# Hashed attention and a gated FFN on one core: turns, hashes, value products and means cut into products and laid out over the slots of the opening; later loads in another order

## The chip, the cores and the metric

The kernel runs on one core of a Trainium2 chip. The metric is the device time of one execution in microseconds (us), from a few runs of the same program; one further execution was taken by the hardware profiler, and every row below is from that one.

## What is computed

The first stage is attention for 4 batches of 8 heads, 768 tokens of 64 numbers, in which a query sees only the keys of its own hash bucket. The second is a feed-forward network with a gate over the 3072 tokens, all in float32:

```python
q_bits = (np.einsum('bhsd,dk->bhsk', q, proj) > 0)       # proj: 64 x 6
k_bits = (np.einsum('bhsd,dk->bhsk', k, proj) > 0)
...
mask = q_bucket[:, :, :, None] == k_bucket[:, :, None, :]
scores = np.where(mask, scale * np.matmul(q, k.transpose(0, 1, 3, 2)), -1e9)
...
attn = attn / (np.sum(attn, axis=-1, keepdims=True) + 1e-09)
x = np.matmul(attn, v)                                   # then heads side by side: 3072 x 512
...
xn = x / np.sqrt(np.mean(x * x, axis=-1, keepdims=True) + 1e-06) * rms_g
g = xn @ w_gate                                          # 512 x 1536
out = (g * sigmoid(g) * (xn @ w_val)) @ w_out            # 1536 x 512
```

## The kernel before

**Windows and slots.** A window w is half of a batch (batch w // 2): 384 queries of all 8 heads. The work is laid out by hand over slots. A slot is one third of one head in one window: scores of 256 keys against the 384 queries (`scores`, two products, L338) and their exponential on ScalarE (`probs`, L349). `SLOTS` (L34) lists them. The first 48 belong to windows 0 and 1, pair of heads by pair of heads in the order of `TURNS` (L33): pair 0 of window 0, pair 0 of window 1, pair 1 of window 0, and so on, except that pairs 2 and 3 of window 0 come before pairs 2 and 3 of window 1. From slot 48 on windows 2 to 7 follow, 24 slots each. Scores have two buffers in PSUM (`scps`).

**The plan.** `at(s, f, ..., rank)` puts a step into slot s. The last loop (L699) emits for each slot s the scores of slot s + 1, the steps of rank under 3, the exponential of slot s + 1, then the other steps by rank and order of entry. Every engine and every DMA queue works through its own instructions in the order in which they were emitted; SyncE's queue carries nearly all loads of q, k and v and the small moves of hash bits, and in the later part the output.

**Preparing a head.** Batch 0 and pairs 0 and 1 of batch 1 (`BY_PE`, L40) are turned by TensorE: `turn_pe` (L161) makes three 128x128 products into one PSUM bank, DVE copies the bank to `kT` or `qT` (`keep`), POOL and ScalarE cast it into `QK` (`casts`, L543). Pairs 2 and 3 of batch 1 and all of batches 2 and 3 are loaded in blocks (`load_blocks`, four DMAs) and turned on DVE (`turn_dve`, L187, four instructions each for k and q) and cast on POOL (`cast_pool`). The hash of two heads is one group of four float32 products of 384 columns, side by side on TensorE (`hash_bank`, L206), followed by one sign operation on DVE (`signs`) that gives +-16 and +-32 in `bits`. Twelve rows of bits per block then go under the 64 rows of the head in `QK` (so that the mask is part of the score product): by DVE copies or by small DMAs on SyncE. `hash_head` (L231) hashes one head of batch 0, `hash_heads` (L253) a pair, `hash_lone` (L273) pairs 2 and 3 of batch 1, with eight moves on SyncE each.

**Values, means, normalization.** `av` (L357) multiplies the exponentials with the values, 18 products a head, in halves of nine in the second and third slot after the head. `v_prep` casts the values; `v_sum` and `v_mean` (L319) give the mean of the values that stands in for the 1e-9. `attn_out` (L374) divides, `sumsq`, `norm`, `scale_x` (L420) and `turn_x` (L425) normalize and turn x. For window 0 this comes at slots 38 to 47, since the network of window 0 begins in slot 48.

**The network.** Twelve `gate` and `value` groups of four products in 16 slots, then `project`. Turns, hashes, means, x turns, gates, values and projections share three PSUM banks (`gps`, tag "g"); each bank is freed by the engine that reads it, DVE for most.

**Loads.** Ten tiles for raw q, k and v (`lpool`). The opening's loads of batch 0 stand ahead of the slots, among them the v of pairs 2 and 3 (L566, L567). The weights are loaded and cast by DMAs of POOL's queue (`load_w`, `load_wo`) in slots 2 to 39.

Of the kernel before, what the change touches and what calls it, by code (L numbers as in the profile page):

```python
# [36 lines left out]
LAST = {(w, h): g for g, (w, h, p) in enumerate(SLOTS) if p == 2}  # L37

# [5 lines left out]
def kernel(  # L44
# [115 lines left out]

    def turn_pe(b, h, which, room=None):  # L161
        hp, hh = divmod(h, 2)
        qk_tile(b, hp)
        if hh == 0:
            t_tile(b, hp, which)
        src = raw[b, hp, which][:, hh].rearrange("p (c e) d -> p c (e d)", e=2)
        ps = bank("t_ps", [128, HALF]) if room is None else room
        for i in range(3):
            nc.tensor.transpose(ps[:, 128 * i : 128 * i + 128], src[:, i], ident)  # L169
        return ps  # L170
# [82 lines left out]
    def hash_heads(b, hp):  # L253

        ps = hash_bank(
            [(w[:, 0:32], t0(b, 2 * hp + hh, which))
             for hh in range(2) for w, which in ((pk, "k"), (pq, "q"))]
        )
        bt = bits_tile(0)
        signs(bt, ps)  # L260

        def move(eng, blocks):
            for hh, t in blocks:
                p0 = 64 * hh + 32 * (t % 2) + 12 * (t // 2)
                dst, src = bit_rows(b, 2 * hp + hh, t), bt[p0 : p0 + 12]
                if eng is nc.sync:
                    eng.dma_start(out=dst, in_=src)  # L267
                else:
                    eng.tensor_copy(dst, src)

        return move
# [47 lines left out]
    def v_mean(b, hp, n, parts=(None,)):  # L319
        hs = slice(2 * hp, 2 * hp + n)  # L320
        ps = bank("m_ps", [128, n, 65])
        for i, jt in enumerate(parts):
            rhs = vsum[b % 2][:, hs, 0:65] if jt is None else vls[b % 2][:, hs, jt, 0:65]
            nc.tensor.matmul(
                ps, ones16, rhs, start=(i == 0), stop=(i == len(parts) - 1)
            )
        nc.vector.tensor_scalar_mul(cvb[b % 2][:, hs, 0:65], ps, C0 / S)
# [29 lines left out]
    def av(w, h, i0, i1):  # L357
# [5 lines left out]
        for i in range(i0, i1):  # L363
            c, jt = divmod(i, 6)
            nc.tensor.matmul(  # L365
                o[:, c, hh, 0:65],
                psb[w, h][:, jt // 2, jt % 2, 128 * c : 128 * c + 128],
                vls[b % 2][:, h, v_chunk(b, h, jt), 0:65],
                start=(hh == 0 and i == 0), stop=(jt == 5),
                skip_group_check=True,  # L370
            )
# [48 lines left out]
    def scale_x(w, c):  # L420
        if w not in xn:
            xn[w] = npool.tile([128, 3, DMODEL], FP16, name="xn")
        nc.vector.tensor_scalar_mul(xn[w][:, c, :], x[w][:, c, :], rstds[w][:, c : c + 1])  # L423
# [142 lines left out]
    load_rows(nc.sync, 0, 2, "v")  # L566
    load_rows(nc.sync, 0, 3, "v")  # L567
# [13 lines left out]
    def hash_one(h):  # L581
        moves[h] = hash_head(h)
        moves[h]((nc.sync,), 3)

    def hash_pair(b, hp):
        moves[b, hp] = hash_heads(b, hp)
        odd = [(0, 2), (1, 2), (0, 3), (1, 3)]
        even = [(0, 0), (0, 1), (1, 0), (1, 1)]
        moves[b, hp](nc.sync, odd if b == 0 else even[:2] + odd[:1] + even[2:] + odd[1:])

# [4 lines left out]
    for hp, turns, sv in ((1, (1, 2, 4, 5), 8), (2, (8, 9, 10, 11), 19), (3, (14, 15, 17, 18), 25)):  # L595
        for i, s in enumerate(turns):
            at(s, keep_pair, 0, hp, i)
            at(s + 1, casts, 0, hp, i)
        at(sv, v_prep, 0, hp)

    for h, s in ((2, 3), (3, 7)):
        at(s, hash_one, h)
        for t in range(3):
            at(s + 1 + t, lambda h=h, t=t: moves[h]((nc.vector,), t), rank=5)
    for hp, s, slots in ((2, 13, (15, 16, 17, 18)), (3, 20, (22, 23, 24, 25))):
        at(s, hash_pair, 0, hp)
        for i, s in enumerate(slots):
            at(s, lambda hp=hp, i=i: moves[0, hp](nc.vector, [divmod(i, 2)]), rank=5)
    for hp, s in enumerate((6, 16, 30, 36)):
        at(s, v_mean, 0, hp, 2, range(6))  # L610
    for i, (t, src) in enumerate(((wg, moe_w_gate), (wv, moe_w_val))):
        at(2 + 4 * i, load_w, t, src, 0, 768)
        at(12 + 9 * i, load_w, t, src, 768, 1536)
        at(33 + 6 * i, load_wo, 6 * i, 6 * i + 6)

    for hp, loads, turns, sv in ((0, (9, 11, 15), (24, 26, 28, 30), 42),
                                 (1, (13, 17, 28), (33, 35, 37, 39), 45)):
        for which, s in zip("kqv", loads):  # L620
            at(s, load_rows, nc.sync, 1, hp, which)
        for i, s in enumerate(turns):
            at(s, keep_pair, 1, hp, i)
            at(s + 1, casts, 1, hp, i)
        at(turns[3] + 2, hash_pair, 1, hp)
        at(sv, v_prep, 1, hp)
        at(sv + 2, v_sum, 1, hp)
# [3 lines left out]
    def in_row(loads, s, hash_slot=None):  # L631
# [3 lines left out]
        (1, 2): ((21, 23, 30), (36, 37, 40, 40, 48, 49, 50, 51), (42, 52, 46), 53),  # L635
        (1, 3): in_row((42, 44, 47), 52, 61),
        (2, 0): in_row((51, 56, 59), 61), (2, 1): in_row((64, 67, 70), 71, 80),
# [20 lines left out]
    at(54, v_mean, 1, 0, 4)  # L658
# [16 lines left out]
    for w in range(8):  # L675
        for h in range(H):
            end = LAST[w, h] + 3
            at(end - 1, av, w, h, 0, 9)
            at(end, av, w, h, 9, 18)
            if h % 2:  # L680
                at(end, o_step, w, h // 2, rank=4.5)
                if (w, h) != (0, 7):
                    at(end + 6, s_step, w, h // 2, rank=5)
        at(end + (1 if w == 0 else 9), norm, w, rank=5)
        for c in range(3):
            at(end + (3 if w == 0 else 14 + c), scale_x, w, c, rank=5)
            at(end + (7 + c if w == 0 else 17 + 2 * c), turn_x, w, c, rank=1)
# [70 lines left out]
```

## Time and profile before

| | us |
|---|---|
| median of 3 runs | 339.33 (337.27, 339.33, 345.63) |
| the profiled execution | 339.3 |
| its span | 337.5 |
| TensorE busy in the span | 326.8 |
| DVE / ScalarE / POOL busy | 236.4 / 210.0 / 155.3 |

A row of the timeline gives start, duration, engine, line, operation, result and operands, shape and count, and in brackets how long the engine was idle before it and what ended that. Rows of equal instructions that follow each other are merged (x4). The ends of matmuls are modelled, so that the distance from one start to the next tells more than the duration. "SPq" is the queue that SyncE issues DMAs from: the duration there is the issuing, not the transfer.

### The profile page before, as it was taken

The page shows a single profiled execution, that of the slowest core. Times are in us where ns is not written, and L with a number is a line of the kernel's source. Part 1 is how long each engine was busy: PE and PEld are TensorE (multiplying, and loading weights), DVE is VectorE, ACT ScalarE, POOL GpSimd, SP SyncE. Part 2 cuts the span into 40 slices and gives each one's busy share as a digit, 9 for nine tenths or more (in the row PEclk, how much of TensorE's full clock was granted, in tenths as well). Part 3 has the DMA queues.
Part 4 walks back from the last instruction along what each step waited for, and adds up shares of the span by engine and source line. Part 5 has one row for each costly group of instructions (what it writes and reads, how often), then busy time and mean ns, then how long its engine had stood idle before and what let it go on. Part 6 is the DMA issues. An engine that isn't in the chain of part 4 may idle for free.

```text
span 337.5 us, 7796 instructions
## 1 busy us (share of the span) xinstructions
PE 326.8 (97%) x2993; PEld 201.0 (60%) x2993; DVE 236.4 (70%) x526; ACT 210.0 (62%) x328; POOL 155.3 (46%) x230
## 2 busy tenths in 40 slices
PE   8999989889999999999999999999999999999995
PEld 7566656455566565566555666566556665655653
DVE  4769798688758896668768897557546663883860
ACT  3789987656666575757666676567667675332321
POOL 4878789836465576245736475613111311110000
PEclk9999999999999999999999999999999999999999
DMA  7999999464376064508243261100010001001002
GB/s 238 330 223 260 169 169 187 75 124 100 79 186 118 15 111 119 104 20 168 69 105 84 44 116 64 35 16 0 33 62 2 3 0 64 33 0 64 32 0 93
DMA packets 80244, 31.36 MB, mean 93 GB/s; under 512 B 65240, under 2 KB 77264, under 8 KB 80208
## 3 DMA queue, kind: packets, MB, share of 16 engines
q1 hardware_dynamic: 76272, 26.09, 31.7%
q0 software_dynamic: 3712, 4.72, 8.8%
q8 instruction: 23, 0.38, 0.5%
q14 instruction: 13, 0.11, 0.1%
q10 hardware_dynamic: 224, 0.07, 0.1%
HBM read 28.32 MB, written 6.29 MB: 103 GB/s over the span
## 4 chain that ended last, share of the span: by engine, by line
PE 85%; DVE 6%; SPq 3%; DMA 2%; ACT 2%; issue 1%; DVEq 0%; ACTq 0%
PE y_ps L469 18%; PE v_ps L455 17%; PE s_ps L343 15%; PE g_ps L445 12%; PE o_ps L365 9%; PE s_ps L445 5%; PE d_ps L209 4%; SPq L267 2%; PE t_ps L169 1%; PE x_ps L430 1%; PE z_ps L336 1%; DMA kL<-in_k_dram 1%; DVE otmp L380 1%; DVE xn L423 1%; ACT psb L353 1%
## 5 line engine op out<-in xcount | busy, mean ns | idle before, releaser
L353 ACT ACTIVATE psb<-s_ps 128x768 f16<-128x768 f32 x192 | 150.8, 808 | 28.1 <-PE s_ps L343 26.9
L343 PE MATMUL s_ps<-QK 76*128 76x384 f16 x384 | 93.5, 325 | 1.3 <-ACT psb L353 0.5
L455 PE MATMUL v_ps<-xnT,wv 128*128 128x384 f16 x384 | 78.1, 326 | 0.1
L469 PE MATMUL y_ps<-wo,ht 128*128 128x512 f16 x276 | 69.2, 379 | 0.3 <-ACT ysb L476 0.3
L389 POOL TENSOR_TENSOR x<-otmp,rcp 128x384 f32<-128x384 f32 x31 | 25.7, 830 | 93.0 <-DVE rcp L385 92.7
L365 PEld LDWEIGHTS <-psb 128*128 128x128 f16 x1152 | 51.6, 97 | 25.5 <-issue 7.5
L447 ACT ACTIVATE t<-g_ps 128x384 f32<-128x384 f32 x72 | 35.3, 490 | 43.6 <-PE g_ps L445 43.4
L458 DVE SCALAR_TENSOR_TENSOR ht<-a,v_ps 128x384 f16<-128x384 f32 x96 | 53.2, 554 | 10.7 <-PE v_ps L455 1.5
L457 DVE SCALAR_TENSOR_TENSOR a<-t,g_ps 128x384 f32<-128x384 f32 x72 | 39.5, 548 | 28.5 <-ACT t L447 28.3
L445 PE MATMUL g_ps<-xnT,wg 128*128 128x384 f16 x288 | 58.6, 325 | 0.7 <-DVE a L457 0.5
L365 PE MATMUL o_ps<-vl,psb 128*128 128x65 f16 x1152 | 56.8, 194 | 0.6 <-DVE otmp L380 0.5
L455 PEld LDWEIGHTS <-wv 128*128 128x128 f16 x384 | 36.4, 97 | 23.9 <-issue 0.5
L445 PEld LDWEIGHTS <-wg 128*128 128x128 f16 x384 | 36.0, 97 | 24.4 <-issue 1.1
L343 PEld LDWEIGHTS <-QK 76*128 76x128 f16 x384 | 31.6, 98 | 16.1 <-issue 3.7
L469 PEld LDWEIGHTS <-ht 128*128 128x128 f16 x276 | 25.9, 97 | 24.0 <-issue 0.6
L476 ACT COPY ysb<-y_ps 128x512 f32<-128x512 f32 x23 | 13.5, 585 | 25.5 <-PE y_ps L469 22.8
L431 DVE TENSOR_TENSOR xnT<-x_ps,gcol 128x512 f16<-128x512 f16 x24 | 16.3, 685 | 15.1 <-PE x_ps L430 15.1
L401 POOL TENSOR_TENSOR sq<-x 128x384 f32<-128x384 f32 x31 | 25.6, 826 | 2.4
L380 DVE TENSOR_TENSOR otmp<-o_ps,cvb 128x390 f32<-128x390 f32 x32 | 17.8, 558 | 8.8 <-PE o_ps L365 8.7
L447 ACT ACTIVATE t<-s_ps 128x384 f32<-128x384 f32 x24 | 11.8, 491 | 18.4 <-PE s_ps L445 17.6
L201 POOL CAST QK<-kT 64x768 f16<-64x768 f32 x20 | 16.8, 838 | 12.4 <-DVE kT L193 6.5
L193 DVE STREAM_TRANSPOSE kT<-kL 128x192 f32<-128x192 f32 x40 | 19.8, 517 | 2.7 <-DMA kL<-in_k_dram 2.7
(80 smaller groups left out, 325.7 us busy)
## 6 DMA issues: line engine op xcount, KB each, us to landing
vL<-in_v_dram SPq DMA_DIRECT2D x16, 384.0 KB
out_dram<-ysb SPq DMA_DIRECT2D x23, 256.0 KB
kL<-in_k_dram SPq DMA_DIRECT2D x40, 96.0 KB
qL<-in_q_dram SPq DMA_DIRECT2D x40, 96.0 KB
kL<-in_k_dram SPq DMA_DIRECT2D x5, 384.0 KB
qL<-in_q_dram SPq DMA_DIRECT2D x5, 384.0 KB
wg<-in_moe_w_gate_dram POOLq DMA_DIRECT2D x2, 768.0 KB, 7.2
wv<-in_moe_w_val_dram POOLq DMA_DIRECT2D x2, 768.0 KB, 8.5
```

The costliest lines, as they stand in the source:

```text
L343: nc.tensor.matmul(ps[:, j, 0:HALF], k_cols(w // 2, h, 2 * p + j), q_cols(w, h), start=True, stop=True,)
L353: nc.scalar.activation(psb[w, h][:, p], sps.pop(g)[:, :, 0:HALF], AF.Exp, scale=ESCALE,)
L365: nc.tensor.matmul(o[:, c, hh, 0:65], psb[w, h][:, jt // 2, jt % 2, 128 * c : 128 * c + 128], vls[b % 2][:, h, v_chunk(b, h, jt), 0:65], s ...
L380: nc.vector.tensor_add(tmp[:, :, :, 0:65], o[:, :, :, 0:65], cvb[b % 2][:, 2 * hp : 2 * hp + 2, 0:65].unsqueeze(1).to_broadcast([128, 3, 2 ...
L389: eng.tensor_mul(xd.rearrange("p c (h d) -> p c h d", h=2), tmp[:, :, :, 0:64], r.to_broadcast([128, 3, 2, 64]),)
L401: nc.gpsimd.tensor_mul(sq, xd, xd)
L445: nc.tensor.matmul(g, wg[:, kt, fs], xnT[w][:, kt], start=(kt == 0), stop=(kt == 3))
L447: nc.scalar.activation(t, g, AF.Tanh, scale=0.5)
L455: nc.tensor.matmul(vv, wv[:, kt, fs], xnT[w][:, kt], start=(kt == 0), stop=(kt == 3))
L457: nc.vector.scalar_tensor_tensor(out=a, in0=t, scalar=1.0, in1=g, op0=ALU.add, op1=ALU.mult)
L458: nc.vector.scalar_tensor_tensor(out=ht[w][:, ft], in0=a, scalar=0.5, in1=vv, op0=ALU.mult, op1=ALU.mult)
L469: nc.tensor.matmul(y, ht[w][:, ft, c * 128 : (c + 1) * 128], wo[:, ft, :], start=(ft == 0), stop=(ft == NF - 1),)
```

## The change

In the opening (slots 0 to 50) pieces take the place of whole steps:

- A turn is made by `turn_part`, product by product; the dictionary `turns` says how many products each slot takes. Pair 1 of batch 1 is turned in slots 39 to 44 (33 to 39 before), pair 0 in slots 27 to 36 (24 to 30).
- A hash is made by `hash_part` in pieces of 128 columns; `hashes` gives for each hash the slots of its three columns. Heads 6 and 7 of batch 0 get a hash each (one for both before). Pairs 0 and 1 of batch 1 are hashed in slots 37 to 39 and 46 to 47 (32 and 41 before).
- `by_dve` names the bit moves that DVE makes and their slots (18, before 14); the others of batch 0 go to SyncE (6, before 10), as do all 16 of batch 1's pairs 0 and 1.
- Means of pairs 1 to 3 of batch 0 are cut in two; values of windows 0 and 1 are multiplied pair by pair in five slots (`av_pair`; four for the last pair of window 0, whose result comes a slot earlier). One of three rows of x of window 0 is scaled on ScalarE.
- Loads: v of pairs 2 and 3 of batch 0 move into slots 17 and 24; q, k, v of batch 1's pairs 0 and 1 from slots 9 to 28 to slots 18 to 40; the output weights from slots 33 and 39 to 47 and 50. Pair 2 of batch 1 is loaded in slots 40, 48, 49 (21, 23, 30 before), turned in 50 to 55 (36 to 51), hashed in 56 (53); pair 3 is loaded in 50, 52, 54 (42, 44, 47), turned in 56 to 61 (52 to 59), hashed in 62 (61); the casts and sums of v go along.

```diff
+    def turn_part(b, h, which, i0, i1):
...
+        ps = tps[b, h, which]
...
+        for i in range(i0, i1):
+            nc.tensor.transpose(ps[:, 128 * i : 128 * i + 128], src[:, i], ident)
+        if i1 == 3:
+            nc.vector.tensor_copy(t0(b, h, which), ps)
...
+    def hash_part(b, heads, i0, i1):
...
+        cs = slice(128 * i0, 128 * i1)
+        for t in range(4):
+            i, j = divmod(t, 2)
+            h, o = (heads[0], 12 * i) if len(heads) == 1 else (heads[i], 0)
+            nc.tensor.matmul(
+                ps[32 * t : 32 * t + 32, cs], (pk, pq)[j][:, o : o + 32],
+                t0(b, h, "kq"[j])[:, cs],
+                start=True, stop=True, tile_position=(0, 32 * t),
+            )
+        if i1 < 3:
+            return
+        bt = bits_tile(0)
+        signs(bt, ps)
...
+    turns = {
+        (0, 1): {1: 3, 2: 3, 3: 6},
+        (0, 2): {9: 1, 10: 2, 11: 2, 12: 2, 13: 4, 14: 1},
+        (0, 3): {19: 1, 20: 2, 21: 3, 22: 3, 26: 2, 27: 1},
+        (1, 0): {27: 2, 32: 1, 33: 3, 34: 3, 35: 2, 36: 1},
+        (1, 1): {39: 1, 40: 2, 41: 2, 42: 2, 43: 4, 44: 1},
+    }
+
+    hashes = {
+        (0, (2,)): (4, 5, 5), (0, (3,)): (6, 8, 9), (0, (4, 5)): (15, 15, 16),
+        (0, (6,)): (23, 24, 25), (0, (7,)): (28, 28, 29),
+        (1, (0, 1)): (37, 38, 39), (1, (2, 3)): (46, 46, 47),
+    }
...
+    by_dve = {
+        (0, 2): {0: 6, 1: 7, 2: 7, 3: 11}, (0, 3): {0: 10, 1: 11, 2: 12, 3: 13},
+        (0, 4): {0: 17, 1: 18}, (0, 5): {0: 18, 1: 19},
+        (0, 6): {0: 26, 1: 26, 2: 27}, (0, 7): {0: 30, 1: 30, 2: 31},
+    }
...
+        if b == 1:
+            for h, t in [(h, t) for h in heads for t in range(3)] + [(h, 3) for h in heads]:
+                at(slots[2], move, nc.sync, b, h, t)
+    for hp, s in ((1, 13), (2, 24), (3, 31)):
+        at(s, v_prep, 0, hp)
+    for hp, s in ((2, 17), (3, 24)):
+        at(s, load_rows, nc.sync, 0, hp, "v")
...
-        at(33 + 6 * i, load_wo, 6 * i, 6 * i + 6)
...
-    for hp, loads, turns, sv in ((0, (9, 11, 15), (24, 26, 28, 30), 42),
-                                 (1, (13, 17, 28), (33, 35, 37, 39), 45)):
+        at(47 + 3 * i, load_wo, 6 * i, 6 * i + 6)
+
+    for hp, loads, sv, ss in ((0, (18, 20, 31), 48, 49), (1, (26, 28, 40), 50, 51)):
...
-        (1, 2): ((21, 23, 30), (36, 37, 40, 40, 48, 49, 50, 51), (42, 52, 46), 53),
-        (1, 3): in_row((42, 44, 47), 52, 61),
-        (2, 0): in_row((51, 56, 59), 61), (2, 1): in_row((64, 67, 70), 71, 80),
+        (1, 2): ((40, 48, 49), (50, 51, 51, 52, 52, 53, 54, 55), (53, 56, 54), 56),
+        (1, 3): ((50, 52, 54), (56, 56, 57, 57, 58, 59, 60, 61), (58, 62, 64), 62),
+        (2, 0): in_row((56, 58, 60), 62), (2, 1): in_row((64, 67, 70), 71, 80),
...
-    at(54, v_mean, 1, 0, 4)
+    at(55, v_mean, 1, 0, 4)
...
+            elif h % 2:
+                cuts = (0, 8, 17, 26, 36) if (w, h) == (0, 7) else (0, 7, 14, 21, 28, 36)
+                for s, i0, i1 in zip(range(end - 4, end + 1), cuts, cuts[1:]):
+                    at(s, av_pair, w, h // 2, i0, i1)
+                end -= (w, h) == (0, 7)
```

149 lines of the change are left out of this document (94 added, 55 removed).

## The prediction

> **What bounds the kernel now.** I read the page first, then busy time by stretch, then TensorE's timeline, the SyncE queue (SPq) and the chain of waits. The run of the profile took 339.3 us, 1.8 us of it outside its span; the median of the three runs is 339.33, so sums against this run need no correction. Stretches (span, then busy time and count of PE, PEld, DVE, ACT, POOL, then clock, DMA share, GB/s), cut where slots begin (below):
>
> ```profile
> span 337.5 us, 7796 instructions
> PE 85%; DVE 6%; SPq 3%; DMA 2%; ACT 2%; issue 1%; DVEq 0%; ACTq 0%
> 9.88:45.81 35.93, 34.08 (x421) 23.41 (x419) 28.57 (x64) 32.45 (x48) 29.71 (x48) 1.00 1.04 229
> 45.81:55.37 9.56, 8.16 (x96) 4.96 (x96) 9.35 (x24) 7.16 (x11) 8.05 (x13) 1.00 1.13 215
> 55.37:85.39 30.02, 27.61 (x257) 16.21 (x253) 23.14 (x52) 18.71 (x30) 20.31 (x29) 1.00 0.55 99
> 85.39:337.50 252.11, 248.31 (x2162) 149.81 (x2158) 170.96 (x360) 147.78 (x235) 92.12 (x122) 1.00 0.26 62
> ```
>
> Behind 85.39 TensorE is all but without gaps (248.3 of 252.1 us), and the change leaves that part alone. So the question is when TensorE gets there. Slot s begins on TensorE with the score pair of slot s+1; counting pairs, slot 1 begins at 9.88 (second pair of the first row below), slots 39, 48 and 65 at the cuts above, 45.81, 55.37 and 85.39:
>
> ```profile
> 9.55 0.82 PE L343 MATMUL s_ps<-QK 76*128 76x384 f16 x4
> ...
> 16.63 0.49 PE L343 MATMUL s_ps<-QK 76*128 76x384 f16 x2
> 17.05 0.51 PE L209 MATMUL d_ps<-kT,pk 128*32 128x384 f32 x1
> ...
> 17.40 0.49 PE L209 MATMUL d_ps<-kT,pk 128*32 128x384 f32 x1
> ...
> 17.84 0.45 PE L365 MATMUL o_ps<-vl,psb 128*128 128x65 f16 x9
> 18.12 0.49 PE L343 MATMUL s_ps<-QK 76*128 76x384 f16 x2
> 18.45 0.49 PE L169 MATMUL t_ps<-ident,kL 128*128 128x128 f32 x3
> 18.78 0.44 PE L365 MATMUL o_ps<-vl,psb 128*128 128x65 f16 x9
> ```
>
> The ends of these rows are modelled; prices are therefore start to next start: score pair 0.33, turn of a head 0.33 (0.11 a product), half of a head's values 0.28, a hash 0.88 (16.63 + 0.33 to 17.84). By these the 38 slots from 9.88 to 45.81 hold 38 pairs 12.5, 19 turns 6.3, 5 hashes 4.4, 24 value halves 6.6, 4 means at 0.35 1.4: 31.2 us of work in 35.9, so 4.7 us idle. It comes in lumps: a slot with a hash needs 1.5 us, one without as little as 0.33.
>
> From slot 39 to 65 another queue sets the pace:
>
> ```profile
> 34.62 6.73 SPq L121 DMA_DIRECT2D kL<-in_k_dram  x4
> 41.45 2.66 SPq L121 DMA_DIRECT2D qL<-in_q_dram  x4
> 44.21 2.34 SPq L111 DMA_DIRECT2D vL<-in_v_dram  x2
> 46.65 14.63 SPq L267 DMA_DIRECT2D QK<-bits  x16
> 61.39 3.06 SPq L121 DMA_DIRECT2D kL<-in_k_dram  x4
> 64.56 2.64 SPq L121 DMA_DIRECT2D qL<-in_q_dram  x4
> 67.30 0.59 SPq L111 DMA_DIRECT2D vL<-in_v_dram  x1
> 67.99 3.05 SPq L121 DMA_DIRECT2D kL<-in_k_dram  x4
> 71.15 6.18 SPq L284 DMA_DIRECT2D QK<-bits  x8
> 77.44 2.71 SPq L121 DMA_DIRECT2D qL<-in_q_dram  x4
> 80.19 0.64 SPq L111 DMA_DIRECT2D vL<-in_v_dram  x1
> 81.62 6.31 SPq L284 DMA_DIRECT2D QK<-bits  x8
> ```
>
> Sixteen issues at 0.77 (71.15 to 77.44 holds eight) are 12.3 of the 14.63, and behind 61.39 SyncE issues without a pause until 80.83. The sixteen bit moves of batch 1's pairs 0 and 1 stand ahead of the k blocks of pair 3 (61.39). DVE waits for those blocks and TensorE behind it, for a bank:
>
> ```profile
> 67.28 0.52 DVE L193 STREAM_TRANSPOSE kT<-kL 128x192 f32<-128x192 f32 x1 [2.73 <-DMA kL<-in_k_dram]
> ...
> 65.84 0.81 PE L455 MATMUL v_ps<-xnT,wv 128*128 128x384 f16 x4
> 68.30 0.29 PE L324 MATMUL m_ps<-vsum,ones 128*128 128x260 f16 x1 [1.65 <-DVE bits L216]
> 69.10 0.81 PE L445 MATMUL g_ps<-xnT,wg 128*128 128x384 f16 x4 [0.51 <-DVE a L457]
> 69.75 0.49 PE L343 MATMUL s_ps<-QK 76*128 76x384 f16 x2
> ```
>
> Four products take 0.65 (69.10 to 69.75, where slot 55 begins), so behind 66.49 TensorE lost about 2.5 us there. The last moves (81.62) carry the bits of pair 3; the first three of them must land before the scores at 85.39, and these start with no recorded wait: just in time.
>
> **The opening, slots 1 to 38.** The value products (216) and means stay the same in number and are only spread. Batch 1's pair 1 leaves, 16 turns instead of 19: -1.0. The hashes become 14 pieces with 17 products of 128 columns, since heads 6 and 7 each get a hash. The two passes of a hash begin 0.35 apart, so 0.70 of its 0.88 goes with the columns and 0.18 stays: a piece costs 0.18 + 0.23 a product, 14 and 17 make 6.5 against 4.4. If the 0.18 hides behind the neighbours the 17 products cost 4.0; if each piece drains as the full hash does, 6.5. I take the upper end, since the row shows it. Work: 31.2 - 1.0 + 2.1 = 32.3. Slots now hold 0.65 to 1.2 us against 0.74 of ACT per exp (below), so most lumps go; I leave 1.9 of the 4.7 us idle, 0 and 4.7 being the ends.
>
> ```profile
> 31.46 5.27 ACT L353 ACTIVATE psb<-s_ps 128x768 f16<-128x768 f32 x7 [0.38 <-PE s_ps L343]
> ```
>
> Seven exps in 5.27 with the last at full length 0.81 are at most 0.74 each; 48 of them and a cast per q turn fit beside TensorE. Slot 39 then begins at 9.88 + 32.3 + 1.9 = 44.1, 1.7 us earlier than now (42.2 to 46.9). The 18 bit copies on DVE (14 before), the extra sign operation and one x row fewer on DVE (now ACT) lie beside this: DVE is busy 28.6 of 35.9. Value loads of pairs 2 and 3 move behind slot 17 and land well before slots 28 and 34; the weight loads of POOL move out of the opening to slots 47 and 50 and are first needed in slot 64. I cost these at nothing, and up to 1 us if the landing of a load is late.
>
> **The later loads, slots 39 to 65.** Here lies the price. Pair (1,0) is hashed in slots 37 to 39 and (1,1) in 46 and 47, and all their 16 moves stay on SyncE. The k, q and v loads of pair 2 and the v of pair 1, which SyncE issued at 34.62 to 46.55 ahead of the moves, now stand in slots 40, 48, 49, that is behind the first or the second eight. From the signs of slot 39 to the third move of the last hash SyncE had 45 issues; now it has 55. Prices from the rows, start to next start: eight moves 6.29, four blocks 2.75 (3.16 where k blocks take longer), v 0.69. Counted from the beginning of slot 39: the signs are done after 0.33 (pair), 0.11 (turn product) and the last piece with its sign operation (a full hash begun at 17.05 has its signs by 18.65 in the row below; less two of three products, 0.47, that is 1.1), together 1.6. Eight moves end at 7.9, v and k blocks at 11.3, the other eight moves at 17.6 (their signs come in slot 47, some 9 us after slot 39 began, so no wait), the q blocks of pair 2 at 20.4. They land 2.8 later, as the k blocks above did (issued by 64.45, used at 67.28): 23.2. The next v, k, q and v are issued by 27.7.
>
> ```profile
> 17.97 0.68 DVE L216 TENSOR_SCALAR bits<-d_ps,thr,scl 128x384 f16<-128x384 f32 x1 [0.54 <-PE d_ps L209]
> ```
>
> DVE meets the first q turn of pair 2 in slot 52. TensorE could be through slot 52 some 16 us after slot 39 (slots 39 to 47: nine pairs 3.0, four turns 1.3, three pieces with four products 1.5, 50 value products 1.5, three x turns 1.0 at most, in all 8.3; slots 48 to 52: five pairs 1.6, eight groups of four products 5.2, 31 value products 0.9, in all 7.7), so DVE stands still for about 6 us, and all adds behind it. TensorE has three banks and runs dry about two slots later. That is the stall of now, longer, and at the same slot: 44.1 + 23.2 = 67.3 against 67.28. The 1.7 us of the opening are gone here.
>
> After it pair 2's hash (slot 56, was 53) is near: slot 55 came 2.5 us after the restart, then 1.4 for slot 55, 1.0 to the hash, 1.6 with signs: 29.7, two behind SyncE's 27.7. Its eight moves end at 36.0, k blocks 39.1, q 41.9, v 42.6, three moves of pair 3's hash (slot 62, was 61) 45.0, landing 1.4 (issued by 84.0 for the scores at 85.39): 46.4. Slot 65 begins at 44.1 + 46.4 = 90.5; without the two us for the signs at 88.5. Now it is 85.39: between +3.1 and +5.1, and I take +4, as the hash's wait shrinks if TensorE has run ahead. 339.3 + 4.0 = 343.3. Its own range: slot 39 at 42.2 with no sign wait gives 42.2 + 44.4 = 86.6, 340.5; a k block group held as at 34.62 (4 us more) reaches 347.
>
> Two edits have one answer: the x row on ACT and the earlier end of head 7 take DVE's chain (x, squares, xn) out of the way of the hash of pair 1, which waited 0.9 us for it; that lies before slot 52 and so inside the wait for SyncE. The order of value products changes no count.
>
> ```profile
> 49.36 0.83 PE L209 MATMUL d_ps<-qT,pq 128*32 128x384 f32 x2 [0.90 <-DVE qT L177]
> ```
>
> **The rivals.**
> A, faster: issuing is not the bound. TensorE's work alone would bring slot 65 at 44.1 + 8.3 + 27.5 (30.0 less the 2.5 stall) + 1 idle = 80.9, 4.5 us early: 334.8. It decides if an issue costs under 0.6 us instead of 0.77 and 0.69, for then the 55 issues with their landings end before TensorE gets there. Against it: the moves at 71.15 and 81.62 cost the same with DMA at 0.55 of its time as the ones at full load. For it: only that DMA is calmer in the new opening. 0.18. The Trainium skill ("DMA: Bandwidth & Descriptors", section "Issuing engines are not separate DMA queues") says that the time a sequencer takes to initiate a DMA is usually small beside the DMA itself; by that rule this rival holds and the time is 334.8. The trace disagrees: 6.18 us for eight small moves one behind the other, with the chain of waits in them.
> B, slower: the opening gains nothing. Waits for banks held over several slots (a turn begun in slot 27 and ended in 32, a hash over four slots) give the 4.7 us idle back: slot 39 at 46.9, the time 346. DVE, which frees the banks, is busy 80% there. 0.12.
> C, slower: the long stall cools TensorE. At the start three transposes took 0.64 (rows below; 0.33 later), so TensorE ran at half speed for about 4 us from 1.04; a second such stage after a stall of some 4.5 us costs 2 us before pair 2's hash: 345.4.
>
> ```profile
> 4.00 0.85 PE L169 MATMUL t_ps<-ident,kL 128*128 128x128 f32 x3
> 4.64 0.85 PE L169 MATMUL t_ps<-ident,qL 128*128 128x128 f32 x3
> ```
>
> Against it: the 2.5 us stall of now slowed nothing (the g products after 69.10 run at 0.65). 0.13. The Trainium skill ("TensorE: Matmul & The Clock Gate", section on the HAM clock gate) halves the clock after an idle window of about 3.4 us; 2.5 us is under that, so the trace neither bears it out nor denies it.
>
> **Chances.** The forecast has 0.57, A 0.18, B 0.12, C 0.13. The likeliest is 343.3. From 335.5 to 347.0 lies all but the lower half of A (0.09) and the upper tails of B, C and the forecast (0.09). The runs shown spread from 337.3 to 345.6, so 2% is about what can be told from no change: under 332.5 only if A comes with an opening free of idle time, 0.04; over 346.1 half of B, a third of C and a tenth of the forecast, 0.16; within, 0.80.
>
> **What would show it.** Right: slot 39 near 44; eight moves, v, k, eight moves, q in an unbroken row on SyncE; DVE waiting 4 us or more for q blocks in slot 52; scores waiting for bits at slot 60 or 65; gaps on TensorE from 60 to 90 of some 9 us in all, and none behind. Wrong: SyncE idle between slots 48 and 62, or slot 65 at or before 85.

## The result: 5.8% slower, and the profile after

The changed kernel took 357.14 us (median of six runs, 355.64 to 360.74) beside 339.35 us for the kernel before (six runs): a ratio of 1.058, 95% interval [1.050, 1.066]. Slower was the right side, but the forecast was 343.3 us with an upper end of 347.0. The profiled execution took 355.64 us, 16.3 us more than that of before. Executions that were slow as a whole are left out of every ratio; of the kernels below that is one of r4's four (679 us) and two of r8's (378 and 1903 us), the profiled ones among them.

The page's first line, the chain of waits by engine, and the TensorE clock that was granted in 40 slices of the span (in tenths; 9 is 90% or more):

```profile
span 353.9 us, 7976 instructions
PE 86%; DVE 6%; DMA 2%; SPq 1%; ACT 1%; issue 1%; POOL 1%; DVEq 0%; POOLq 0%; ACTq 0%
PEclk9999899959999999999999999999999999999999
```

The shares of the chain hardly differ from before, so they tell nothing. The clock row does: it was 9 in all 40 slices, and now dips in slices 5 (35 to 44 us) and 9 (71 to 80). Busy time by stretch, cut at the beginnings of slots 1, 39, 48 and 65 as in the prediction (span, length, then busy time and count of PE, PEld, DVE, ACT, POOL, then clock, DMA share, GB/s):

```profile
9.65:49.93 40.28, 37.29 (x484) 23.77 (x482) 29.24 (x64) 32.63 (x47) 27.27 (x44) 0.96 0.80 186
49.93:59.92 9.99, 8.38 (x121) 5.95 (x118) 8.24 (x22) 8.51 (x13) 6.28 (x12) 1.00 0.04 9
59.92:102.02 42.10, 30.44 (x261) 17.62 (x257) 26.98 (x61) 18.25 (x30) 25.47 (x36) 0.88 0.79 136
102.02:353.90 251.88, 248.29 (x2156) 149.69 (x2156) 169.06 (x355) 147.77 (x235) 90.88 (x120) 1.00 0.26 62
```

The last row is that of before to 0.2 us. The opening went from 35.93 to 40.28 us and slots 48 to 65 from 30.02 to 42.10 us, each with a clock below 1. TensorE begins these slots, worked out from its timeline as in the prediction:

| slot | before | after | difference | forecast |
|---|---|---|---|---|
| 15 | 24.98 | 22.98 | -2.00 | |
| 16 | 25.64 | 25.59 | -0.05 | |
| 27 | 35.39 | 35.19 | -0.20 | |
| 30 | 37.91 | 42.10 | +4.18 | |
| 39 | 45.81 | 49.93 | +4.11 | -1.7 |
| 52 | 61.47 | 65.80 | +4.33 | |
| 53 | 63.37 | 76.41 | +13.04 | |
| 64 | 83.91 | 97.35 | +13.44 | |
| 65 | 85.39 | 102.02 | +16.63 | +4 |
| 71 | 94.23 | 110.86 | +16.62 | |

So 2 us are won ahead of slot 15, and time is lost at four places: 2.0 us in slot 15, 4.4 in slots 27 to 29, 8.7 in slot 52 and 3.2 in slot 64.

**Slot 15.** DVE's timeline, then one row of TensorE's:

```profile
20.46 1.69 DVE L307 COPY QK<-bits 12x384 f16<-12x384 f16 x3
...
23.64 0.74 DVE L307 COPY QK<-bits 12x384 f16<-12x384 f16 x1
24.42 0.56 DVE L177 COPY qT<-t_ps 128x384 f32<-128x384 f32 x1
```

```profile
25.03 0.62 PE L284 MATMUL d_ps<-qT,pq 128*32 128x256 f32 x2 [0.75 <-DVE qT L177]
```

The hash of heads 4 and 5 begins one slot after the end of the last turn. It needs the copy of that turn, and this stands on DVE behind copies of bits for heads 2 and 3, the last of which need not stand there (r5 below).

**Slots 27 to 29.** TensorE, DVE and POOL in the same stretch:

```profile
36.53 0.41 PE L175 MATMUL t_ps<-ident,kL 128*128 128x128 f32 x2 [0.73 <-DMA kL<-in_k_dram]
...
38.99 0.63 PE L284 MATMUL d_ps<-qT,pq 128*32 128x256 f32 x1 [1.18 <-DVE qT L177]
```

```profile
36.21 1.67 DVE L307 COPY QK<-bits 12x384 f16<-12x384 f16 x2
37.91 0.56 DVE L466 TENSOR_REDUCE ssp<-sq 128x3 f32<-128x384 f32 x1
38.38 0.55 DVE L177 COPY qT<-t_ps 128x384 f32<-128x384 f32 x1
```

```profile
36.15 0.82 POOL L345 CAST vl<-vL 128x768 f16<-128x768 f32 x1
36.94 0.83 POOL L450 TENSOR_TENSOR x<-otmp,rcp 128x384 f32<-128x384 f32 x1
```

First the k rows of batch 1's pair 0, loaded nine slots later than before, are late. Then the same order bites again: two copies of 9 KB take 1.67 us, each ending about 0.1 us after the POOL operation beside it, and the turn's copy waits behind them. What these gaps do to the clock follows here (stretches of one us):

```profile
36.00:37.00 1.00, 0.47 (x4) 0.36 (x4) 0.97 (x2) 0.53 (x1) 0.94 (x3) 1.00 1.16 261
37.00:38.00 1.00, 0.81 (x4) 0.14 (x2) 0.96 (x3) 0.70 (x1) 0.92 (x2) 1.00 1.13 220
38.00:39.00 1.00, 0.01 (x2) 0.01 (x3) 0.97 (x3) 0.14 (x2) 0.67 (x1) 0.99 1.15 206
39.00:40.00 1.00, 1.00 (x7) 0.19 (x7) 0.21 (x1) 0.48 (x1) 0.87 (x2) 0.50 1.14 229
...
42.00:43.00 1.00, 1.00 (x19) 0.77 (x17) 0.94 (x3) 0.34 (x2) 0.00 (x0) 0.80 0.38 128
43.00:44.00 1.00, 1.00 (x19) 0.78 (x15) 0.41 (x3) 1.00 (x2) 0.00 (x0) 1.00 0.10 34
```

From 39.0 to about 42.4 TensorE ran at half clock. By the length that costs half of it, some 1.7 us (an estimate).

**Slot 52.** SyncE's queue, POOL's issues of the output weights, then who waits:

```profile
52.66 6.08 SPq L305 DMA_DIRECT2D QK<-bits  x8
58.84 0.46 SPq L112 DMA_DIRECT2D vL<-in_v_dram  x1
59.40 3.15 SPq L122 DMA_DIRECT2D kL<-in_k_dram  x4
62.65 11.76 SPq L305 DMA_DIRECT2D QK<-bits  x8
74.52 2.70 SPq L122 DMA_DIRECT2D qL<-in_q_dram  x4
```

```profile
60.02 0.94 POOL L592 DMA_DIRECT2D wo<-in_moe_w_out_dram  x1
...
63.81 0.86 POOL L592 DMA_DIRECT2D wo<-in_moe_w_out_dram  x1
```

```profile
73.81 0.52 DVE L211 STREAM_TRANSPOSE kT<-kL 128x192 f32<-128x192 f32 x1 [8.42 <-DMA QK<-bits]
...
79.54 0.87 DVE L211 STREAM_TRANSPOSE qT<-qL 128x192 f32<-128x192 f32 x2 [1.52 <-DMA qL<-in_q_dram]
```

```profile
75.18 1.44 PE L521 MATMUL v_ps<-xnT,wv 128*128 128x384 f16 x4 [7.96 <-DVE a L523]
76.41 0.84 PE L386 MATMUL s_ps<-QK 76*128 76x384 f16 x2
77.05 1.48 PE L511 MATMUL g_ps<-xnT,wg 128*128 128x384 f16 x4
```

The k blocks of pair 2 were issued by 62.55, and DVE could turn them at 73.81, 11 us later. The output weights, issued from 60.02 on, are in the queues with them. The profile names a move of bits as the releaser; that the blocks landed just then is read from SyncE, whose last two moves use the semaphores of the third and fourth block again and were issued at 72.71 and 73.70 only. DVE stood still for 8.4 us with the gate product that frees TensorE's bank (line 523) queued behind, and TensorE ran dry for 8 us. After that four products take 1.2 to 1.3 us from start to start instead of 0.65: half clock, until about 79.9.

**Slot 64.** The scores wait for the bits of pair 3's hash, the last group of moves in SyncE's row:

```profile
102.02 0.48 PE L386 MATMUL s_ps<-QK 76*128 76x384 f16 x2 [3.03 <-DMA QK<-bits]
```

### The profile page after: what moved, and what is told of

Same layout as the page of the kernel before. It is cut to its first block, busy times and chain, and to the rows that moved or that the text cites. A ratio compares the mean times of both kernels' runs of the same rounds, so it can differ in the third digit from the quotient of the medians.

```text
span 353.9 us, 7976 instructions
## 1 busy us (share of the span) xinstructions
PE 332.6 (94%) x3081; PEld 203.2 (57%) x3081; DVE 237.8 (67%) x530; ACT 211.1 (60%) x329; POOL 155.0 (44%) x230
## 3 DMA queue, kind: packets, MB, share of 16 engines
HBM read 28.32 MB, written 6.29 MB: 98 GB/s over the span
## 4 chain that ended last, share of the span: by engine, by line
PE 86%; DVE 6%; DMA 2%; SPq 1%; ACT 1%; issue 1%; POOL 1%; DVEq 0%; POOLq 0%; ACTq 0%
PE v_ps L521 17%; PE y_ps L535 17%; PE s_ps L386 16%; PE g_ps L511 13%; PE o_ps L408 8%; PE s_ps L511 4%; PE d_ps L227 3%; PE o_ps L426 2%; PE d_ps L284 2%; DMA QK<-bits 2%; PE x_ps L496 1%; DVE QK L307 1%; SPq L305 1%; PE t_ps L175 1%; PE z_ps L379 1%
## 5 line engine op out<-in xcount | busy, mean ns | idle before, releaser
L386 PE MATMUL s_ps<-QK 76*128 76x384 f16 x384 | 95.0, 329 | 5.5 <-DMA QK<-bits 3.0
L521 PE MATMUL v_ps<-xnT,wv 128*128 128x384 f16 x384 | 79.0, 328 | 8.0 <-DVE a L523 8.0
L408 PEld LDWEIGHTS <-psb 128*128 128x128 f16 x864 | 39.5, 98 | 19.5 <-issue 4.1
L408 PE MATMUL o_ps<-vl,psb 128*128 128x65 f16 x864 | 43.0, 194 | 0.0
```

Of the source, the lines that this page charges most:

```text
L386: nc.tensor.matmul(ps[:, j, 0:HALF], k_cols(w // 2, h, 2 * p + j), q_cols(w, h), start=True, stop=True,)
L408: nc.tensor.matmul(o[:, c, hh, 0:65], psb[w, h][:, jt // 2, jt % 2, 128 * c : 128 * c + 128], vls[b % 2][:, h, v_chunk(b, h, jt), 0:65], s ...
L521: nc.tensor.matmul(vv, wv[:, kt, fs], xnT[w][:, kt], start=(kt == 0), stop=(kt == 3))
```

## The experiments

Times are compared by the ratio to the kernel before run beside them on the same chip. The last three columns come from each profiled run: the beginning of slot 39 against that of before (45.81), the time from there to slot 65, and from slot 65 to 71, behind which the traces differ by 0.4 us at most.

| kernel | ratio | slot 39 | 39 to 65 | 65 to 71 |
|---|---|---|---|---|
| before | 1 | 0 | 39.58 | 8.84 |
| after | 1.058 | +4.1 | 52.09 | 8.84 |
| r1: after, later loads as before | 1.024 | +7.5 | 41.18 | 8.84 |
| r2: after, output weights early | 1.051 | +2.6 | 51.62 | 11.87 |
| r3: after, pair 2 loaded early | 1.034 | +4.2 | 44.86 | 8.84 |
| r5: after, five moves to SyncE | 1.068 | +7.2 | 51.91 | 8.84 |
| r6: r3, row of x on DVE | 1.031 | +3.0 | 43.96 | 8.84 |
| r9: before, pair 3's k two slots early | 1.012 | +0.7 | 42.48 | 8.84 |
| r10: before, later loads as after | 1.058 | +8.7 | 46.76 | 10.33 |
| r11: r9, lone moves half on DVE | 1.014 | 0 | 41.09 | 9.12 |
| r12: r6, lone moves half on DVE | 1.024 | +4.3 | 40.02 | 11.60 |
| r13: r12, opening mended | 1.016 | +0.7 | 40.00 | 12.95 |
| r14: r13, v of pair 3 rounded early | 1.008 | +0.3 | 40.65 | 9.12 |
| r15: r14, lone copies spread | 1.016 | -0.2 | 42.03 | 8.84 |

r4 and r8 have ratios (1.061 and 1.058) but no trace that can be read.

The column on slot 39 is coarse. Slot 1 itself begins anywhere from 9.22 to 10.57 us in these traces (9.89 before), and a stretch of half clock in the opening is there in some (after, r1, r3, r5, r10, r12) and not in others. r3 and r6, which are the same up to slot 39, differ by 1.3 us in it.

**The later loads back (r1).** All loads, turns and hashes of pairs 2 and 3, the loads of batch 1's pairs 0 and 1 and the output weights in the slots of before:

```diff
-        at(47 + 3 * i, load_wo, 6 * i, 6 * i + 6)
+        at(33 + 6 * i, load_wo, 6 * i, 6 * i + 6)
-    for hp, loads, sv, ss in ((0, (18, 20, 31), 48, 49), (1, (26, 28, 40), 50, 51)):
+    for hp, loads, sv, ss in ((0, (9, 11, 15), 42, 44), (1, (13, 17, 28), 45, 47)):
-        (1, 2): ((40, 48, 49), (50, 51, 51, 52, 52, 53, 54, 55), (53, 56, 54), 56),
+        (1, 2): ((21, 23, 30), (36, 37, 40, 40, 48, 49, 50, 51), (42, 52, 46), 53),
...
```

> The changed opening (turns, hashes, values, means as changed) with every later load, turn, cast and hash of pairs 2 and 3 of batch 1, the loads of pairs 0 and 1, v_sum and the output weights in the slots of before. Theory L (the later order costs the 12 us between slots 48 and 66, the opening only its 4.5 us): 344 to 345 us, slot 48 near 60, slot 65 some 30 us later. Rival O (the late hashes of pairs 0 and 1 alone crowd SyncE): 350 or more, with the stall in slot 52 still there.

Measured: 345.99 us, ratio 1.0245 [1.0191, 1.0300], a microsecond above what was expected. From slot 39 to 65 it lost 1.6 us instead of 12.5, so 11 us of the loss belong to the later loads. But slot 39 came 7.5 us late, not 4.1: with the old loads the new opening is worse still, as TensorE waits 2.8 us for DVE's copies of q turns and 0.9 us for a value rounding (line 345) whose load now stands behind pair 2's blocks on SyncE. Not all of the 7.5 us is told apart: slot 1 began 0.9 us later than in the changed kernel, and half clock lasted from 40.8 to 47.7.

**The output weights early (r2).** Only the first line of that diff.

> The changed kernel with the output weights' two loads back in slots 33 and 39. Theory W (these 3 MB take the DMA engines from pair 2's k blocks): the k blocks land 3 us after issue, the eight moves behind them go out in 6 us and not in 11.8; if that is all, the 8.7 us of slot 52 shrink to under 3 and the time is 349 or less. Theory Q (SyncE's order sets it): q blocks still stand behind eight moves, DVE waits for them until some 24 us after slot 39, and the time is 351 to 353.

Measured: 355.01 us, ratio 1.0513 [1.0464, 1.0562], above both times that were expected. SyncE and DVE in this trace:

```profile
58.39 4.21 SPq L122 DMA_DIRECT2D kL<-in_k_dram  x4
62.70 6.47 SPq L305 DMA_DIRECT2D QK<-bits  x8
69.28 2.70 SPq L122 DMA_DIRECT2D qL<-in_q_dram  x4
```

```profile
64.83 0.53 DVE L211 STREAM_TRANSPOSE kT<-kL 128x192 f32<-128x192 f32 x1 [0.36 <-DMA kL<-in_k_dram]
...
74.97 0.86 DVE L211 STREAM_TRANSPOSE qT<-qL 128x192 f32<-128x192 f32 x2 [5.88 <-DMA qL<-in_q_dram]
```

Now k blocks issued by 62.60 are turned at 64.83, 2.2 us later instead of 11, and the eight moves behind them take 6.47 us instead of 11.76. The stall of slot 52 is gone (slot 53 at +3.6 instead of +13.0). So the traffic of the output weights was its cause. But the time barely falls, since the next stall is the one forecast: DVE waits 5.88 us for the q blocks, issued behind the moves. It comes at slot 55, costs 7.2 us there and leaves TensorE at half clock until 82.4; a wait of 3.8 us for bits at slot 64 does so once more. Slot 39 to 65 takes 51.6 us, as with the weights in the way. Two causes cover each other here, and taking one away shows the other.

**Pair 2 early (r3).** Its loads in slots 32, 34 and 41 take both away:

```diff
-        (1, 2): ((40, 48, 49), (50, 51, 51, 52, 52, 53, 54, 55), (53, 56, 54), 56),
+        (1, 2): ((32, 34, 41), (50, 51, 51, 52, 52, 53, 54, 55), (53, 56, 54), 56),
```

> The changed kernel with only the loads of pair 2 of batch 1 moved ahead of both sets of eight moves (k, q, v in slots 32, 34, 41 instead of 40, 48, 49). Theory Q: no wait for blocks of pair 2, slot 53 at 4.5 us behind before as slot 52, time 345 to 348. Theory W: the output weights still hold the DMA engines, moves and the blocks of pair 3 come late instead, time 351 or more.

Measured: 349.29 us, ratio 1.0342 [1.0298, 1.0387], 1 us above what theory Q had; 7.2 us less from slot 39 to 65. What is left there is 5.3 us of waits for bits (three, the longest 2.9) and half clock behind the longest. In the changed kernel these loads stood behind the bits of slots 39 and 47; their place in the queue alone was worth 7 us.

**The hashes of the opening later (r4).** Those of heads 4 and 5 and of head 7 by one slot, so that DVE's copies are ready:

```diff
-        (0, (2,)): (4, 5, 5), (0, (3,)): (6, 8, 9), (0, (4, 5)): (15, 15, 16),
-        (0, (6,)): (23, 24, 25), (0, (7,)): (28, 28, 29),
+        (0, (2,)): (4, 5, 5), (0, (3,)): (6, 8, 9), (0, (4, 5)): (16, 16, 17),
+        (0, (6,)): (23, 24, 25), (0, (7,)): (29, 29, 30),
```

> The changed kernel with the hash of heads 4 and 5 in slots 16, 16, 17 and that of head 7 in 29, 29, 30, one slot behind now; nothing else. Theory H (the first piece follows the last turn product so closely that TensorE waits for DVE's copy of it): the 2 us at slot 15 and 3 to 4 us at slots 28 to 30 go, no half clock there, slot 39 at 45 to 46 and the time 351 to 353. Rival D (DVE is behind anyway, and k of pair (1,0) late): slot 39 moves by under 1.5 us, time 355 to 357.

Measured: 358.1 to 359.0 us in three executions, ratio 1.0611 [1.0564, 1.0658]: nothing gained, and above both times that were expected. Why stays open, as there is no trace to read.

**The early copies off DVE (r5).** The last moves of heads 2 and 3 and three of head 6 go by SyncE:

```diff
-        (0, 2): {0: 6, 1: 7, 2: 7, 3: 11}, (0, 3): {0: 10, 1: 11, 2: 12, 3: 13},
+        (0, 2): {0: 6, 1: 7, 2: 7}, (0, 3): {0: 10, 1: 11, 2: 12},
...
-        (0, 6): {0: 26, 1: 26, 2: 27}, (0, 7): {0: 30, 1: 30, 2: 31},
+        (0, 7): {0: 30, 1: 30, 2: 31},
```

> The changed kernel with five bit moves taken from DVE and given to SyncE: the last of heads 2 and 3 (slots 11 and 13) and the first three of head 6 (slots 26, 26, 27). Theory D (DVE's bit copies, 0.25 us alone but up to 0.87 beside POOL, stand ahead of its copies of the turns, for which the next hash waits): slot 16 comes 1 to 1.3 us earlier, the step from slot 28 to 30 shrinks from 5.3 to 2 or 2.5, slot 39 moves from 49.9 to some 46, and as SyncE's row starts there the time falls by as much: 352 to 353 of 357. Rival K (the late k of pair (1,0) and the half clock hold slot 28): the step stays over 4, time 355 or more.

Measured: 361.13 us, ratio 1.0678 [1.0620, 1.0735]. The half that concerns heads 2 and 3 came out: slot 16 begins 1.3 us earlier than in the changed kernel, and the step from slot 15 to 16 falls from 2.6 to 1.2 us. The other half turned round:

```profile
33.74 3.59 SPq L305 DMA_DIRECT2D QK<-bits  x4
```

```profile
41.24 0.80 PE L386 MATMUL s_ps<-QK 76*128 76x384 f16 x2 [4.44 <-DMA QK<-bits]
```

Four moves of 9 KB issued by 37.33 landed 4 us later, and the scores waited 4.4 us. Six loads of 384 KB were issued on the same queue between 29.05 and 38.39, and one of 768 KB by POOL. Slot 39 lies at +7.2.

**The row of x back on DVE (r6).** r3 with all three rows of x of window 0 scaled on DVE.

```diff
-        if (w, c) == (0, 1):
+        if False:
```

> The kernel with pair 2's loads early (r3), with the second row of x of window 0 scaled on DVE again. If ScalarE, which waits for the norm ahead of that row, holds the exponentials: the step from slot 42 to 43 falls from 2.4 to under 1.2 and the time of 349.3 by about 1 us; if DVE has no room for it: the x turns at slots 45 to 48 come later by as much and nothing is gained, 349 to 350.

Measured: 348.01 us, ratio 1.0314 [1.0259, 1.0369]. The step from slot 42 to 43, 2.4 us in r3, is 0.76: on ScalarE the row stood ahead of an exp and waited for rstd, the factor of the normalization, from POOL. But 1.2 us are given back in slot 45, so from slot 39 to 48 the edit gains 0.45 us. Most of the rest of what the two traces differ by lies ahead of slot 39, where the edit changes nothing, and the intervals of the two ratios overlap: that the time came out about 1 us lower, as expected, is in part luck.

**The later loads alone (r8, and r10 once more).** The kernel before with the lines that r1 took back:

> The kernel before with only the later order of the change: loads, turns, casts, hashes of pairs 2 and 3 of batch 1, loads and sums of pairs 0 and 1, output weights; turns and hashes of the opening as before (hashes of pairs 0 and 1 in slots 32 and 41). Theory Q (SyncE's order): the sixteen moves go out earlier than in the changed kernel, but pair 2's blocks now stand behind the first eight or all of them: 3 to 6 us slower than before, most of it in slots 50 to 66. Rival (the later order is harmless, the late hashes do the harm): within 1 us of before. Rival W (output weights in slots 47 and 50 hold the blocks whatever stands ahead): 8 us or more.

> The kernel before with the new order of the later loads, turns and hashes only. If the later order alone carries the loss, as its time of 357 us says, the trace has the opening of before (slot 39 near 46, slot 48 near 55.5) and loses in two places: one stall of 6 to 10 us between slots 50 and 56, with the values of pair 2 waiting for VectorE's rounding and that for the turns of late k blocks, and 2 to 4 us of waits for bits between slots 59 and 65. The rival, that this order delays the opening through the loads of pairs 0 and 1 that it also moved, has slot 39 at 49 or later.

Measured: ratio 1.0580 [1.0509, 1.0651] in r8, where 3 to 6 us were expected, and one run of 356.65 us in r10. The time equals that of the whole change, but not for the reason expected in r10: slot 39 is at +8.7, as the rival had it, since the turns of before are in slots 24 to 30 and the q rows, now loaded in slot 20, aren't there for the one in slot 26.

```profile
42.06 0.90 PE L169 MATMUL t_ps<-ident,qL 128*128 128x128 f32 x3 [7.10 <-DMA qL<-in_q_dram]
```

Behind slot 39 it loses 7.2 us up to slot 65 and 1.5 more up to slot 71. So this pair of runs does not show what the later loads cost beside the opening for which they were made; r1 and r3 do.

**Pair 3's k blocks earlier (r9, r11).** The wait at slot 54 of the kernel before, which the prediction had found, tested on that kernel; r11 also makes half of the lone hashes' moves on DVE:

```diff
-        (1, 3): in_row((42, 44, 47), 52, 61),
+        (1, 3): in_row((40, 44, 47), 52, 61),
...
+                if hh == 0:
+                    nc.vector.tensor_copy(dst, bt[p0 : p0 + 12])
```

> The kernel before with one load moved: the k blocks of pair 3 of batch 1 from slot 42 to 40, that is between the two sets of eight moves. DVE's wait of 2.7 us at 64.5 and TensorE's of 2.5 us behind it go in any case. Theory Q (SyncE's row of issues sets when slot 65 begins, 85.4): the time falls by less than 1 us, the gain is given back as a wait for bits at slot 60 or 65. Rival (slot 65 had slack): 2 to 2.5 us faster.

> The kernel before with the k blocks of pair 3 two slots earlier, and four of the eight moves of pair 3's two lone hashes as VectorE copies instead of SyncE transfers. If SyncE's row of issues is what makes the scores of slots 59 and 65 wait for bits, the row is shorter by four issues of 0.7 to 0.8 us ahead of each of them, the waits go, and the time is 334.5 to 336 us, 2 to 3 us below the kernel before. If the bits come late for another reason (their signs, or the transfers that share the DMA engines), the time stays at the 342 us of the kernel with the earlier k blocks alone.

Measured: 342.48 us, 1.0122 [1.0063, 1.0180], and 343.24 us, 1.0135 [1.0086, 1.0185]; both are slower than the kernel before, while r9 was expected to be faster by either theory. In r9 slot 55 comes 2.2 us earlier against slot 54 than before, and four slots later the scores wait for bits, with half clock after it:

```profile
77.97 0.48 PE L343 MATMUL s_ps<-QK 76*128 76x384 f16 x2 [3.49 <-DMA QK<-bits]
78.29 1.34 PE L455 MATMUL v_ps<-xnT,wv 128*128 128x384 f16 x4
```

In r11 no wait for bits is left, so SyncE's row was their cause; but TensorE now waits 3.7 us in two waits for DVE's gate products (line 459). The forecast of 334.5 to 336 us fell, and the time is close to the other theory's 342 without its reason: the wait changed its engine.

**Mending the changed kernel step by step (r12 to r15).** r12 is r6 with half of the lone moves on DVE. r13 then mends the opening at the two places seen above:

```diff
-        (0, 2): {0: 6, 1: 7, 2: 7, 3: 11}, (0, 3): {0: 10, 1: 11, 2: 12, 3: 13},
+        (0, 2): {0: 6, 1: 7, 2: 7}, (0, 3): {0: 10, 1: 11, 2: 12},
...
-        (0, 6): {0: 26, 1: 26, 2: 27}, (0, 7): {0: 30, 1: 30, 2: 31},
+        (0, 6): {0: 27, 1: 27, 2: 28}, (0, 7): {0: 30, 1: 30, 2: 31},
...
-    for hp, loads, sv, ss in ((0, (18, 20, 31), 48, 49), (1, (26, 28, 40), 50, 51)):
+    for hp, loads, sv, ss in ((0, (14, 15, 31), 48, 49), (1, (26, 28, 40), 50, 51)):
```

> The changed kernel with the loads of pair 2 in slots 32, 34 and 41, the means' row of ones on VectorE, and half of the lone hashes' moves on VectorE. If SyncE's row is what holds the bits, some 5 us of waits between slots 53 and 66 go and the time is 342 to 344 us, against 348 us with SyncE's moves; slot 65 then lies 1 to 3 us behind the kernel before. If not, 347 us or more.

> As the one above, and the opening mended at the two places where its trace waits: the last moves of heads 2 and 3 go by SyncE, those of head 6 are one slot later on VectorE, and the loads of pair 2 of heads 0 to 3 in batch 1 are issued in slots 14 and 15. If the late copies of VectorE and the late k blocks are what the opening loses by, slot 39 lies near 46 and the time is 338 to 340 us. If the opening is bound by what VectorE has to do in all, slot 39 stays at 48 or later and the time at 342 us or more.

(The row named in the first text is the row of x of r6; the loads named in the second are k and q of batch 1's pair 0.)

Measured: 346.65 us, 1.0244 [1.0184, 1.0304], and 343.70 us, 1.0161 [1.0104, 1.0217]. Both times missed what was expected, while the places did what was expected: in r12 slot 39 to 65 takes 40.0 us instead of r6's 44.0, in r13 slot 39 lies at +0.7 instead of +4.3. Some of the latter is half clock, 3.4 us long in the opening of r12 and absent in r13. Each gave part of it back behind slot 65, in one wait on TensorE (r13):

```profile
90.76 0.27 PE L367 MATMUL m_ps<-vsum,ones 128*128 128x260 f16 x1 [2.31 <-POOL vsum L355]
```

The change had moved the rounding of pair 3's values, which POOL sums after it, from slot 61 to 64, two slots ahead of the mean; as long as TensorE came late, nobody saw it. r14 moves it back, and r15 spreads DVE's four copies behind each lone hash over three slots:

```diff
-        (1, 3): ((50, 52, 54), (56, 56, 57, 57, 58, 59, 60, 61), (58, 62, 64), 62),
+        (1, 3): ((50, 52, 54), (56, 56, 57, 57, 58, 59, 60, 61), (58, 62, 61), 62),
```

> The last kernel above with the values of pair 3 of batch 1 rounded in slot 61 instead of 64, as in the kernel before. In the last trace the mean of that pair, in slot 66, waits 2.3 us on TensorE for GpSimd's sum of these values, and slots 66 to 69 lose 4.1 us. If the moved rounding is what loses there, the trace loses under 1 us in these slots and the time is 339 to 341 us. If the sum only takes GpSimd from other work that is due then, the loss moves to slots 61 to 65 and the time stays at 342 us or more.

> As r14, with VectorE's four copies of bits behind each lone hash put into three slots instead of one. In the trace with all four together they take 1.57 us in slot 56 and TensorE waits 1.8 us behind them for VectorE in slots 57 and 59, and 4.1 us are lost from slot 55 to slot 60. If the burst is the cause, 2 to 4 us of these come back and the time is 336 to 338.5 us, that of the kernel before. If VectorE is simply full there, the waits stay and the time is that of r14 within 1 us.

Measured: 341.00 us, 1.0083 [1.0048, 1.0118], as expected for r14: that wait is gone. r15 has 342.87 us, 1.0158 [1.0118, 1.0198]: the waits for DVE shrink from 1.8 to 0.7 us, and 2.8 us of waits for POOL's squares come up in their place. In both traces DVE is busy for 5.7 of the 6 us from 72 to 78. What was expected of r15 fell.

Five edits (pair 2's loads, the row of x, the lone moves, the opening, the rounding) thus take the ratio from 1.058 to 1.008. None of these kernels beats the one before. In r14 slots 1 to 39 still take 36.4 us against 35.9.

## Why the prediction was wrong

**The row on SyncE.** Right as a mechanism. From 52.66 on SyncE issued almost without a pause, and slot 65 waited for its last group of moves. It was forecast to begin 46.4 us after slot 39 at most, and began 52.1 after it. Two terms were mis-sized: the first eight moves began 2.7 us after slot 39 instead of 1.6, and the second eight took 11.76 instead of 6.29. Of these 6.6 us, 1.4 came back at the hash of slot 56, whose signs the row waited for by 0.6 us instead of 2.0.

**"I cost these at nothing."** This is the first of two steps that failed. The prediction moved the issues of the output weights past no queue and asked only when the weights are needed (slot 64). It didn't ask what travels beside them: the k blocks of pair 2, which came 11 us after their issue (2.2 us in r2), and the moves behind them. A load's price was its effect on the others. It is not all, though: with the weights out of the way (r2) the stretch from slot 39 to 65 still takes 51.6 us, not 46.4. There the first moves began 3.1 us after slot 39, the four k blocks took 4.2 us to issue instead of 2.75, and SyncE waited 3.0 us, not 2.0, for the signs of slot 56, behind the stall and its half clock. The forecast had no term for half clock; it stood in rival C alone. The upper end of the range had 4 us for a group of blocks held up; the second eight moves alone lost 5.5. The same sentence priced a late load at up to 1 us in the opening; the wait recorded for it is 0.7 us, but it opens the gaps of slots 27 to 29.

**The stall for q blocks.** It was put at slot 52 and about 6 us (the prediction's own 23.2 and 16 give 7.2). In the changed kernel the k blocks stall there first, and q blocks cost DVE 1.5 us. r2 shows the forecast stall itself, 5.88 us of DVE, 26.5 us after slot 39 began instead of 23.2.

**The opening, "I leave 1.9 of the 4.7 us idle".** This is the second step: slot 39 came at 49.9 instead of 44.1. The work of the pieces was priced about right: a one-product piece begins 0.36 us ahead of what follows it, against 0.18 + 0.23. What failed is the sentence that the 18 copies "lie beside this", argued from DVE's mean of 28.6 us in 35.9. DVE's order decides: a copy of bits ahead of a turn's copy delays the hash, whatever the mean is. Slot 15 shows it: without two of these copies the step to slot 16 falls from 2.6 to 1.2 us (r5, r13). In slots 27 to 29 that is not shown apart: r13 loads the k rows earlier and moves the copies at once, and its opening has no half clock; together that gives 2.2 us. With the mends slots 1 to 39 take 36.4 us, level with the 35.9 of before and not 1.7 us shorter, so the gain forecast from spreading is in no run.

**The row of x on ScalarE** was said to take work out of DVE's way. It made ScalarE wait for rstd ahead of an exp; without it slots 39 to 48 take 0.45 us less (r6).

**Rival C** happened, though not alone: half clock for 3.4 us in the opening and for 4.8 us of TensorE's work after slot 52. By the two lengths that is about 1.7 + 2.4 us, an estimate. Rival A's condition, cheap issues, isn't met in any trace: eight moves in a row took SyncE 6.0 us or more, 0.75 each. Rival B's sign was right (slot 39 late), its mechanism, waits for banks, isn't what the rows name: TensorE waited for a turn's copy and for k rows.

**Signs named in advance.** The row on SyncE, the wait for bits at slot 65 and nothing behind it were right; slot 39 near 44 and the q blocks at slot 52 were wrong.

In sum, slot 65 was forecast at 44.1 + 46.4 = 90.5 without the hash's waits shrinking, and came at 49.93 + 52.09 = 102.02: the two terms are off by nearly equal parts, 5.8 and 5.7 us.

## What to carry to other kernels

A load that is moved must be priced by what travels beside it at its new place: 1.5 MB of weights that were needed only in slot 64 held up four small blocks by 9 us. For small operations on a shared engine ask what stands behind them in the queue, not how busy the engine is. And where several late steps cover each other, undoing one gives little or nothing back (r2: 2 us of 18); judge by the place where the time is lost before and after, and undo them one on top of the other.

## What the runs showed of the hardware

**Small copies on DVE beside POOL.** A copy of 12x384 in f16 takes 0.25 us in the changed kernel's trace with POOL idle (three in 0.79, below), and up to 0.87 beside it (the two of 36.21 above):

```profile
28.34 0.79 DVE L307 COPY QK<-bits 12x384 f16<-12x384 f16 x3
```

The two end at 37.08 and 37.88, 0.11 us after POOL's operations, which end at 36.97 and 37.77. The Trainium skill ("SBUF — State Buffer", section "SBUF: two separate sides") says that the port pair which VectorE shares with GpSimd "is an exclusive lock, not a bandwidth split" for a VectorE operation in a 2-port mode. The rows agree with a lock; no run here took POOL's work away to test it.

**The clock.** The changed kernel's trace has TensorE's clock rise to full at 4.85 us, fall to half at 38.98, rise at 42.40, fall at 69.70 and rise at 79.94. The fall at 69.70 lies within the long wait, 2.5 us after its beginning (columns as above):

```profile
66.00:68.00 2.00, 1.22 (x15) 0.79 (x14) 0.00 (x0) 1.24 (x3) 1.92 (x3) 1.00 1.43 217
68.00:70.00 2.00, 0.00 (x0) 0.00 (x0) 0.00 (x0) 0.17 (x1) 1.06 (x3) 0.93 1.40 212
```

All distances between these times are whole multiples of 3.41 us (10, 1, 8 and 3), and it is so in each of the 14 traces that can be read. What fits them all is that the work of TensorE within each such window decides. A window at full clock that held up to 1.50 us of work (by the modelled ends) was always followed by half clock, one that held 1.82 us or more never, and between the two both occur: 1.79 (r5) fell, 1.72 (the stall in the kernel before) did not. No long gap is needed. Ahead of 38.98 none was over 1.2 us, but the window held 1.50 us of work. r3 and r6 have nearly the same waits there; r3's windows cut them so that one held 1.50 us, and its clock fell, while r6's had 2.15 at the least, and its clock did not. The Trainium skill ("TensorE: Matmul & The Clock Gate", section "Part 1: The HAM clock gate") says that the clock is halved after an idle window of about 3.4 us. The length agrees with this case; that the window must be idle does not, as a window half filled was enough.

**Small transfers behind large ones.** Scores that waited for moves of 9 KB began 1.5 us after the third of these was issued in the changed kernel's slot 64 (100.52 to 102.02), and about 4 us after the last in r5, beside six loads of 384 KB. Blocks of 96 KB were turned 2.2 us after their issue in r2, and 11 us after it beside the output weights in the changed kernel.
